# A first piece of w_in asked for earlier, and two of its quarters loaded as 120 and 8 partitions

## The chip, the core and the metric

The kernel runs on one NeuronCore of a Trainium2 chip. Five engines work side by side: PE (matrix products, TensorE), DVE (VectorE), ACT (ScalarE), POOL (GpSimd) and SP (SyncE), and 16 DMA engines move data between the chip's main memory (HBM) and the on-chip memory. DMAs are asked for by POOL (their packets stand in the profile as queue q0, software_dynamic), by SP (q1) and by ACT (q10); all run on the same 16 engines. The metric is the device time of one execution in microseconds (us), the median of several runs.

## What is computed

The inputs are `x` (8 batches, 8 heads, 512 rows, 64 columns), `state` (8, 8, 32, 64), and two weight matrices `w_in` (512 x 2048) and `w_out` (2048 x 512), all fp32. The reference is a cross attention in both directions, whose outputs are stacked and go through a two-layer network:

```python
scores = scale * x @ state.T ;  a = softmax(scores) ;  xread = a @ state
scores2 = scale * state @ x.T ; a2 = softmax(scores2) ; sread = a2 @ x
rows = concatenate([xread, sread])        # heads side by side: 4352 rows of 512
h = rows @ w_in ;  out = maximum(0.01 * h, h) @ w_out
```

## The kernel before, in words

The kernel never forms `xread`: for each batch it computes `M = state @ w_in` per head (`a_m`, line L389, into PSUM tile `pm`, evicted into the bf16 tile `M`), and then the first layer is `M` times the transposed probabilities `aT` (`ff1`, L410; for batch 0 `ff1_0`, L639). The activation is done on the way out of PSUM by ACT into `hT`, and the second layer (`piece`, L438) multiplies `hT` with `w_out_bf`. The output rows are copied to `ysb` and stored.

The order of the instructions on each engine is written out by hand; each engine works through its own list, and semaphores hold it where an operand is not there.

The stretch that matters here is the head, some 25 us at the start, in which batch 0 goes through a path of its own while the weights arrive:

- SP asks for batch 0's `x` in four transfers of 256 KB (`xf`, L65), and ACT for the first two batches of `state` (`st0f`, L59).
- POOL builds the tables of the head: the identity `ident` (`make_identity`), and in one tile `zeroed` (L76) a regrouped identity `identg` (copies L82 and L86) and the four blocks of ones, `ones4` (memsets L91). PE needs `identg` for the transposes of state (L178, `pst`), `ident` for those of `x` (L487, `pxth`), and `ones4` for the row sums (L548, `r`).
- After the tables POOL asks for fourteen transfers in this order: the four column quarters of `w_in` (`load_w_in`, L145; each 1 MB of fp32, written as 512 KB of bf16), rows 0 to 1 of sixteen of `w_out` (L151), the two halves of batch 1's `x` (`x1`, L573, shown in the trace as `x`), `w_out` rows 2 to 3 and 4 to 7, a half of batch 2's `x` (`xl`, L106), `w_out` rows 8 to 11, the other half, and the rest of `w_out`.
- Eight semaphores count these transfers in turn, so POOL's ninth DMA waits until its first has landed, the tenth until the second, and so on.
- DVE casts `xf` to bf16 (L139), PE transposes and multiplies, and the softmax of batch 0 runs over small steps: the maxima (L527), their split into two bf16 parts `hi` (L535) and `lo` (L538), exponentials on ACT (L543), sums (L548), reciprocals (L558), their spread over rows (`qb`, L517) and the product (L566).
- PE's list then has, in this order: `pm` of quarter 0 for batches 0 and 1, `pm` of quarter 1, the first six column blocks of the first layer, `pm` of quarter 2, four more blocks, scores again, `pm` of quarter 3, six more blocks (L639, outputs `php` and `ph`; ACT evicts them in L651 and L647), a first part of the second layer for batch 0 (`pyw`, L438), the transposes of batch 1's `x` (L705, `pxt`, in two groups of eight; DVE has cast `x1` before that, L687), and then the second layer of batch 0 mixed with batch 1's attention.

From there on PE works through batch after batch with hardly a gap.

Of the kernel before, what the change touches and what calls it, by code (L numbers as in the profile page):

```python
# [9 lines left out]
P = 128  # L10
B, H, S, D = 8, 8, 512, 64
NS = 32
DFF = 2048
DM = 512
SROW = S + NS
NT = S // P
NK = H // 2
SCALE = 1.0 / (D ** 0.5)

BF16 = mybir.dt.bfloat16  # L20
# [7 lines left out]
def kernel(  # L28
# [9 lines left out]
    nc = tc.nc  # L38

    consts = ctx.enter_context(tc.tile_pool(name="consts", bufs=1))  # L40
    wpool = ctx.enter_context(tc.tile_pool(name="wpool", bufs=1))
# [27 lines left out]
    warm = consts.tile([P, 2], FP32, name="warm")  # L69
    nc.vector.memset(warm[:], 0.0)  # L70
    nc.scalar.activation(out=warm[:], in_=warm[:], func=AF.Exp)
    ident = consts.tile([P, P], BF16, name="ident")
    make_identity(nc, ident[:])
    NI = 2 * (P - NS)
# [5 lines left out]
    for g in range(2):  # L80
# [6 lines left out]
            identg[:, g, D:].rearrange("p (k q) -> p k q", k=NK), heads[:, 1, :, g]  # L87
        )

    for c in range(NK):  # L90
        nc.gpsimd.memset(ones4[NS * c:NS * (c + 1), c:c + 1], 1.0)  # L91

    w_in_bf = wpool.tile([P, NK, DFF], BF16, name="w_in_bf")
    w_out_bf = wpool.tile([P, 16, DM], BF16, name="w_out_bf")
    xs, xt, xl = {}, {}, {}

    def load_x(b, eng):
# [39 lines left out]
    def cast_x0(q, copy):  # L137
        v = q % 2
        copy(  # L139
            xs[0][q // 2][:, :, 2 * v:2 * v + 2].rearrange("p t h d -> p h t d"),  # L140
            xf[q][:].rearrange("p h (t d) -> p h t d", t=NT),
        )

    def load_w_in(c):
        nc.gpsimd.dma_start(  # L145
            w_in_bf[:, :, DM * c:DM * (c + 1)],
            moe_w_in[:, DM * c:DM * (c + 1)].rearrange("(k p) f -> p k f", p=P),
        )

    def load_w_out_rows(j0, j1):  # L150
        nc.gpsimd.dma_start(  # L151
            w_out_bf[:, j0:j1, :], moe_w_out[P * j0:P * j1, :].rearrange("(j p) f -> p j f", p=P)
        )
# [411 lines left out]
    def probs0(u):  # L565
        nc.vector.tensor_tensor(out=a0.aT[:, u], in0=e10[u][:], in1=qb0[u][:], op=ALU.mult)  # L566

    for c in range(4):
        load_w_in(c)
    load_w_out_rows(0, 2)  # L570
    x1 = [consts.tile([P, NK, 2 * P], FP32, name="x1", tag=f"x1{u}") for u in range(2)]
    for u in range(2):
# [13 lines left out]
    for q in range(2):  # L586
        cast_x0(q, VEC)
        x0_t(q)
        if q == 0:
            st1_evict()  # L590
            spin(1, "py", S // 2)
    scores0(0)
    cast_x0(2, VEC)
    x0_t(2)
    scores0(1)
    cast_x0(3, VEC)
    x0_t(3)
    max0(0)
# [291 lines left out]
```

## Time and profile before

| what | value |
|---|---|
| median of three runs | 217.58 us |
| the three runs | 217.41, 217.58, 219.19 us |
| span of the profiled execution, first to last instruction | 214.6 us |
| PE busy | 206.1 us, 96% of the span |
| TensorE clock granted | full in all 40 slices |

The profile's page gives the profiled execution as its span alone; its full time is not listed beside it. The median is 2.98 us above the span, which is what lies around the first and the last instruction, as far as this execution was like the median one.

In the profile, "DMA" in a bracket behind a row names a transfer that ended the engine's idle time. A row of the timeline holds the start and the length in us, the engine, the line, the operation, what it writes and reads, and how many instructions were merged.

### The profile page before, as it was taken

What the parts mean: (1) busy time and instruction counts of PE and PEld (TensorE: products, weight loads), DVE (VectorE), ACT (ScalarE), POOL (GpSimd) and SP (SyncE); (2) the same over time, 40 slices, a digit from 0 to 9 for tenths busy, and PEclk for the clock granted to TensorE, in tenths of its full rate; (3) what the DMA queues carried; (4) which work ended last, traced back from release to release, by engine and by line L of the source; (5) the groups of instructions that cost most, each with busy time, mean ns of one, the idle gap of its engine ahead of it and who ended that gap; (6) DMA issues with size and microseconds to landing.
All of it is one profiled execution on the core that took longest, in us unless ns stands there. A gap on an engine that the chain in (4) does not pass through costs nothing.

```text
span 214.6 us, 3685 instructions
## 1 busy us (share of the span) xinstructions
PE 206.1 (96%) x1479; PEld 96.5 (45%) x1504; DVE 97.7 (46%) x149; ACT 139.1 (65%) x263; POOL 25.4 (12%) x39
## 2 busy tenths in 40 slices
PE   7789999999999999999999999999999999999993
PEld 2533434344454444444444444444444455466542
DVE  2666687698748235741784095706580000000001
ACT  3578675898788476856696579647774756464420
POOL 8724100030032040521000000000000000000000
PEclk9999999999999999999999999999999999999999
DMA  6999999576992987394216321422124110111113
GB/s 205 207 206 295 257 253 113 126 270 124 241 217 79 200 243 244 89 276 89 87 52 138 59 99 52 100 47 101 48 68 79 74 74 2 49 52 49 49 49 101
DMA packets 38400, 27.70 MB, mean 129 GB/s; under 512 B 24560, under 2 KB 33136, under 8 KB 38384
## 3 DMA queue, kind: packets, MB, share of 16 engines
q1 hardware_dynamic: 32864, 18.95, 35.4%
q0 software_dynamic: 5376, 8.39, 17.4%
q8 instruction: 12, 0.20, 0.4%
q10 hardware_dynamic: 144, 0.13, 0.3%
q14 instruction: 4, 0.03, 0.1%
HBM read 17.30 MB, written 8.91 MB: 122 GB/s over the span
## 4 chain that ended last, share of the span: by engine, by line
PE 86%; DMA 7%; POOL 3%; ACT 1%; issue 1%; DVE 0%; POOLq 0%; ACTq 0%
PE py L438 50%; PE ph L410 22%; DMA x<-in_x_dram 7%; PE ph L421 3%; PE pm L389 3%; PE pyw L438 3%; PE psr L362 2%; PE pyh L462 2%; POOL w_in_bf L145 1%; PE sc L253 1%; ACT M L403 0%; ACT hT L415 0%; POOL x L573 0%; POOL w_out_bf L151 0%; DVE xb L687 0%
## 5 line engine op out<-in xcount | busy, mean ns | idle before, releaser
L438 PE MATMUL py<-w_out_bf,hT 128*128 128x512 bf16 x446 | 116.7, 380 | 1.0
L415 ACT ACTIVATE hT<-ph 128x512 bf16<-128x512 f32 x112 | 66.5, 602 | 41.7 <-PE ph L410 41.0
L438 PEld LDWEIGHTS <-hT 128*128 128x128 bf16 x496 | 46.7, 98 | 57.2 <-issue 5.3
L410 PE MATMUL ph<-aT,M 128*128 128x512 bf16 x221 | 64.9, 379 | 0.2
L410 PEld LDWEIGHTS <-M 128*128 128x128 bf16 x224 | 21.7, 98 | 27.1 <-issue 1.4
L447 ACT COPY ysb<-py 128x512 f32<-128x512 f32 x31 | 18.1, 585 | 10.7 <-PE py L438 10.7
L263 DVE TRANSPOSE_TENSOR_REDUCE mrow<-sc 128x32 f32<-128x1024 f32 x7 | 8.8, 1250 | 33.7 <-PE sc L253 33.7
L467 DVE COPY ysh<-pyh 128x384 f32<-128x384 f32 x1 | 0.6, 557 | 49.0 <-PE pyh L462 49.0
L132 POOL CAST xb<-xl 128x2048 bf16<-128x2048 f32 x5 | 9.4, 1890 | 58.9 <-DMA xl<-in_x_dram 48.2
L285 DVE TRANSPOSE_TENSOR_REDUCE r<-e 128x32 f32<-128x1024 bf16 x7 | 8.7, 1245 | 11.9 <-ACT e L280 11.9
L403 ACT CAST M<-pm 128x1024 bf16<-128x1024 f32 x13 | 13.2, 1013 | 1.2 <-PE pm L389 0.7
L319 ACT ACTIVATE e<-sc,mcol 128x512 bf16<-128x512 f32 x16 | 11.2, 706 | 0.0
L313 DVE TENSOR_REDUCE mcol<-sc 128x2 f32<-128x1024 f32 x8 | 9.7, 1214 | 0.0
L425 ACT ACTIVATE hs<-ph 128x256 bf16<-128x256 f32 x16 | 6.0, 384 | 4.6 <-PE ph L421 4.4
L294 DVE STREAM_TRANSPOSE qb<-qh 128x1024 bf16<-128x1024 bf16 x7 | 8.7, 1245 | 0.2
L271 DVE STREAM_TRANSPOSE mrowb<-mrow 128x1024 f32<-128x1024 f32 x7 | 8.7, 1245 | 0.2
L273 DVE TENSOR_TENSOR sh<-sc,mrowb 128x1024 f32<-128x1024 f32 x7 | 8.6, 1225 | 0.2
L401 DVE CAST M<-pm 128x512 bf16<-128x512 f32 x10 | 6.4, 686 | 4.9 <-PE pm L389 4.9
L403 DVE CAST M<-pm 128x1024 bf16<-128x1024 f32 x7 | 8.5, 1215 | 0.0
L421 PE MATMUL ph<-sr_t,w_in_bf 128*128 128x256 bf16 x64 | 8.3, 273 | 0.0
L438 PE MATMUL pyw<-w_out_bf,hT 128*128 128x512 bf16 x31 | 7.7, 380 | 0.1
L389 PE MATMUL pm<-w_in_bf,st_t 64*32 64x512 bf16 x192 | 7.6, 379 | 0.0
(97 smaller groups left out, 158.0 us busy)
## 6 DMA issues: line engine op xcount, KB each, us to landing
out_dram<-ysb SPq DMA_DIRECT2D x31, 256.0 KB, 2.4
xl<-in_x_dram SPq DMA_DIRECT2D x3, 1024.0 KB, 6.6
w_in_bf<-in_moe_w_in_dram POOLq DMA_DIRECT2D x4, 512.0 KB, 10.4
xl<-in_x_dram POOLq DMA_DIRECT2D x2, 1024.0 KB, 6.7
xf<-in_x_dram SPq DMA_DIRECT2D x4, 256.0 KB, 3.8
w_out_bf<-in_moe_w_out_dram POOLq DMA_DIRECT2D x4, 256.0 KB, 13.9
x<-in_x_dram POOLq DMA_DIRECT2D x2, 512.0 KB, 15.3
w_out_bf<-in_moe_w_out_dram POOLq DMA_DIRECT2D x2, 512.0 KB, 15.4
```

What stands on the lines that cost most here:

```text
L132: nc.gpsimd.tensor_copy(xt[b][:].rearrange("p t h d -> p h t d"), xl[b][:].rearrange("p h (t d) -> p h t d", t=NT),)
L263: nc.vector.tensor_reduce(out=m1[:], in_=flat.rearrange("p (c j) -> p c j", j=NS), axis=AX.X, op=ALU.max, apply_transpose=True,)
L271: nc.vector.transpose(m1b[:], m1[:, :, None].to_broadcast([P, n, NS]))
L313: nc.vector.tensor_reduce(out=a.m2[:], in_=a.sc[:], axis=AX.X, op=ALU.max, negate=True)
L319: nc.scalar.activation(out=a.e2[:, g], in_=a.sc[:, g, :], func=AF.Exp, bias=a.m2[:, g:g + 1], accum_out=a.r2[:, g:g + 1],)
L389: nc.tensor.matmul(at[v][NS * r:NS * (r + 1)], lhsT=st_of(a, g, k), rhs=w_in_bf[D * g:D * (g + 1), k, DM * c:DM * (c + 1)], start=True, st ...
L403: copy(a.M[:, :, cols], pm[:])
L410: nc.tensor.matmul(ph[:], lhsT=a.M[:, g, P * j:P * (j + 1)], rhs=a.aT[:, g, :], start=(g == 0), stop=(g == 1),)
L415: nc.scalar.activation(out=hT[:, j, :], in_=ph[:], func=AF.Prelu, scale=1 / SCALE, alpha=0.01)
L421: nc.tensor.matmul(ph[:, :n], lhsT=w_in_bf[:, k, P * j:P * (j + 1)], rhs=sr_t[:, k, :], start=(k == 0), stop=(k == NK - 1),)
L438: nc.tensor.matmul(y.py, lhsT=hT[:, j, P * i:P * (i + 1)], rhs=w_out_bf[:, j, :], start=(j == 0), stop=(j == 15),)
L447: copy(ysb[:], ys[b, i].py)
```

## The change

`w_in_bf` and `w_out_bf` are created before the tables, and `load_w_in` takes ranges of row blocks (k), partitions (p) and columns (f). Quarter 0 is now loaded in three transfers: 128 partitions by 256 columns of row block 0, asked for by POOL before `make_identity`; the other 256 columns of that block and the row blocks 1 to 3, asked for after the copies of the tables and ahead of the four memsets of `ones4`. Quarters 1 and 2 are each loaded in two transfers, partitions 0 to 119 and partitions 120 to 127. Quarter 3 is loaded as before. So POOL issues eighteen DMAs in the head where there were fourteen: eight for `w_in`, then the same ten as before in the same order. The eight semaphores are now all taken by `w_in`, and the first transfer of `w_out` waits for the first piece, the halves of `x1` for the second and the third, and so on. The instructions on PE, ACT, DVE and SP are the same and in the same order.

```diff
+    w_in_bf = wpool.tile([P, NK, DFF], BF16, name="w_in_bf")
+    w_out_bf = wpool.tile([P, 16, DM], BF16, name="w_out_bf")
+    wv = moe_w_in.rearrange("(k p) f -> p k f", p=P)
+
+    def load_w_in(c, k0=0, k1=NK, p0=0, p1=P, f0=0, f1=DM):
+        cols = slice(DM * c + f0, DM * c + f1)
+        nc.gpsimd.dma_start(w_in_bf[p0:p1, k0:k1, cols], wv[p0:p1, k0:k1, cols])
+
+    load_w_in(0, 0, 1, f1=DM // 2)
     ident = consts.tile([P, P], BF16, name="ident")
     make_identity(nc, ident[:])
...
+    load_w_in(0, 0, 1, f0=DM // 2)
+    load_w_in(0, 1)
     for c in range(NK):
         nc.gpsimd.memset(ones4[NS * c:NS * (c + 1), c:c + 1], 1.0)
 
-    w_in_bf = wpool.tile([P, NK, DFF], BF16, name="w_in_bf")
-    w_out_bf = wpool.tile([P, 16, DM], BF16, name="w_out_bf")
...
-    def load_w_in(c):
-        nc.gpsimd.dma_start(
-            w_in_bf[:, :, DM * c:DM * (c + 1)],
-            moe_w_in[:, DM * c:DM * (c + 1)].rearrange("(k p) f -> p k f", p=P),
-        )
...
-    for c in range(4):
-        load_w_in(c)
+    for c in range(1, 3):
+        load_w_in(c, p1=P - 8)
+        load_w_in(c, p0=P - 8)
+    load_w_in(3)
     load_w_out_rows(0, 2)
```

## The prediction

> **What bounds the kernel now.** I read the page first: whether an engine is full over the whole span, and what the chain that ended last is made of.
>
> ```profile
> span 214.6 us, 3685 instructions
> PE 206.1 (96%) x1479; PEld 96.5 (45%) x1504; DVE 97.7 (46%) x149; ACT 139.1 (65%) x263; POOL 25.4 (12%) x39
> PE 86%; DMA 7%; POOL 3%; ACT 1%; issue 1%; DVE 0%; POOLq 0%; ACTq 0%
> ```
>
> PE is full, and the change takes no work from it. What can move is the 10% of the chain that is DMA and POOL. The chain in order of time, cut to the first 30 us, says where that lies:
>
> ```profile
> 2.89 3.09 POOL w_in_bf L145 x4
> 7.40 15.65 DMA x<-in_x_dram
> 23.07 0.69 DVE xb L687
> 23.82 0.62 PE pxt L705 x8
> 27.10 2.32 PE py L438 x10
> ```
>
> The second half of `x1` is asked for at 7.40 and lands 15.65 us later, at 23.05. DVE casts it, PE transposes it at 23.82, and behind that PE runs on. So the change is worth what it moves the second `pxt` group. The timeline of PE, and that of ACT, give the waits ahead of it:
>
> ```profile
> 12.76 0.41 PE L389 MATMUL pm<-w_in_bf,stbd 64*32 64x512 bf16 x8 [0.24 <-DMA w_in_bf<-in_moe_w_in_dram]
> 14.20 1.67 PE L639 MATMUL ph<-aT,M 128*128 128x512 bf16 x7
> 16.39 0.41 PE L389 MATMUL pm<-w_in_bf,stbd 64*32 64x512 bf16 x8 [0.52 <-DMA w_in_bf<-in_moe_w_in_dram]
> 17.62 1.04 PE L639 MATMUL ph<-aT,M 128*128 128x512 bf16 x4
> 18.58 0.41 PE L253 MATMUL sc<-xT,stbd 64*32 64x512 bf16 x8
> 17.80 1.02 ACT L651 ACTIVATE hT<-php 128x1024 bf16<-128x1024 f32 x1 [0.42 <-PE php L639]
> 20.35 1.02 ACT L651 ACTIVATE hT<-php 128x1024 bf16<-128x1024 f32 x1 [0.55 <-PE php L639]
> 21.27 2.06 ACT L647 ACTIVATE hT<-ph 128x512 bf16<-128x512 f32 x4
> 22.89 0.61 PE L705 MATMUL pxt<-ident,xb 128*128 128x128 bf16 x8
> ```
>
> PE waits for quarter 1 (0.24), for quarter 2 (0.52) and for `x1`. How the transfers come in is read from the DMA view by window, in its count of packets under 512 B: each DMA engine ends its share of a transfer with a tiny mark. The four rows are the windows 7.8:8.7, 9.7:9.9, 12.9:13.8 and 15.4:15.6; the last row is the instruction queue in 12.5:14.
>
> ```profile
> DMA packets 191, 0.18 MB, mean 200 GB/s; under 512 B 15, under 2 KB 191, under 8 KB 191
> DMA packets 39, 0.04 MB, mean 195 GB/s; under 512 B 1, under 2 KB 39, under 8 KB 39
> DMA packets 186, 0.18 MB, mean 195 GB/s; under 512 B 15, under 2 KB 186, under 8 KB 186
> DMA packets 40, 0.04 MB, mean 195 GB/s; under 512 B 2, under 2 KB 40, under 8 KB 40
> q8 instruction: 1, 0.02, 3.7%
> ```
>
> Fifteen engines are through with quarter 0 by 8.7, the sixteenth only at about 9.8; with quarter 2 fifteen by 13.8, while the last mark falls between 15.4 and 15.6 (the other there belongs to a fast engine that is already through with quarter 3). One engine is some 1.2 us late from the first quarter on and about 2 us late after a 0.02 MB instruction fetch has gone through one engine between. A transfer counts as landed when its last engine is done: PE's wait for quarter 2 ends at 16.39, some 2 us after the other fifteen.
>
> **What the change can give back.** Take the late engine out of the way and see what is late next. The wait for quarter 1 goes: 0.24. The first `ph` run ends at 14.20 + 1.67 = 15.87, and quarter 2's products start at 16.39; without a wait such a group starts a little before the run ahead is drained (the scores at 18.58, where the run ahead ends at 17.62 + 1.04 = 18.66: 0.08), so 0.52 + 0.08 = 0.60 is there. For the second `pxt` group, ACT is next: it must have emptied the PSUM tile, which its row ends at 21.27 + 2.06 = 23.33, so the group could start at 23.38 instead of 23.82: 0.44. ACT can follow, since it is idle for 0.42 and 0.55 in this stretch. Sum: 0.24 + 0.60 + 0.44 = 1.28 us, the most that the head can give. Behind it, `w_out` rows 4 to 7 are due: this DMA row, of the issue at 10.46, gives 16.2 us to landing.
>
> ```profile
> w_out_bf<-in_moe_w_out_dram POOLq DMA_DIRECT2D x1, 512.0 KB, 16.2
> ```
>
> It lands at 26.7; the chain's run of ten from 27.10 is two matmuls on older rows and eight on these, so they are needed at 27.10 + 2 x 0.23 = 27.56. That is 0.9 us of slack, enough for a gain below that, and the late engine's delay falls there too.
>
> **The split quarters.** Quarter 2 as 120 and 8 partitions takes the late engine out if shares go by partition, eight to an engine, and the late engine is the one with partitions 120 to 127. It then has nothing to do in the transfer of 120. Its saving per quarter, from the rate of the stream:
>
> ```profile
> 4.00:5.00 1.00, 0.92 (x13) 0.51 (x13) 0.47 (x1) 0.23 (x1) 1.00 (x2) 1.00 1.06 374
> 8.00:9.00 1.00, 0.18 (x4) 0.25 (x4) 0.73 (x3) 0.01 (x1) 0.92 (x2) 1.00 1.23 203
> 2.00:3.00 1.00, 1.00 (x4) 0.43 (x3) 0.00 (x0) 0.67 (x2) 0.89 (x9) 1.00 0.78 192
> ```
>
> The last number is GB/s written. At 203 GB/s an engine writes a 1 KB row of `w_in` in 1024 x 16 / 203 = 81 ns; a quarter is 512 such rows, 32 to an engine, 2.6 us. Sparing it twice saves 5.2 us against a lag of about 2: enough. The price is the eight partitions: 32 rows per quarter, on eight engines four each, 2 x 4 x 81 ns = 0.65 us on those engines. The fifteen prompt engines then set the landing of `x1`: 23.05 less some 2 plus 0.65 is 21.7, and the cast of 0.69 ends at 22.4, ahead of the 23.38 at which ACT lets PE go on. So on the DMA side nearly the whole 1.28 comes in reach.
>
> No row numbers the engines. The Trainium skill ("DMA: Bandwidth & Descriptors", section "Latency and other measured facts") says that engines 7 and 15 are usually slower than the others. The trace agrees that it is one engine, but shows it late, not slow: its marks for quarters 0 and 2 lie 5.7 us apart and the others' windows 5.1, with a fetch between. By that rule alone the late engine would be the last share's in one case of two, which would make the gain below an even bet.
>
> **The first piece.** Its 128 rows of 512 B are read as 1 KB each, 8 to an engine. Beside `xf`, which moves 374 GB/s in 4:5, a read of 1 KB costs an engine 44 ns, so the piece delays `xf` by at most 0.35 us; it delays it by nothing if it falls into the window 2:3, where the engines move only 192 GB/s. Every step of batch 0's softmax hangs on `xf`, as this row of DVE shows for the last of the four. Queue q0 has no row in the window 4:5; its row in 5:6 stands first below, so its first packets come over 2 us after its first issue at 2.83, and a piece issued near 0.7 would move at about 3, at the edge of the free window. I take 0.2.
>
> ```profile
> q0 software_dynamic: 75, 0.08, 47.7%
> 6.46 0.46 DVE L139 CAST xb<-xf 128x512 bf16<-128x512 f32 x1 [0.24 <-DMA xf<-in_x_dram]
> 2.40 0.49 POOL L91 MEMSET zeroed<- 32x1 bf16 x4
> 2.83 3.15 POOL L145 DMA_DIRECT2D w_in_bf<-in_moe_w_in_dram x4
> 8.14 0.78 POOL L151 DMA_DIRECT2D w_out_bf<-in_moe_w_out_dram  x1
> 10.46 0.78 POOL L151 DMA_DIRECT2D w_out_bf<-in_moe_w_out_dram  x1 [1.54 <-DMA w_in_bf<-in_moe_w_in_dram]
> 4.28 0.44 PE L178 MATMUL pst<-zeroed,stb 128*64 128x96 bf16 x8
> 10.54 0.25 PE L548 MATMUL r<-zeroed,e 128*128 128x4 bf16 x4
> 7.74 0.48 DVE L535 CAST hi<-m 128x16 bf16<-128x16 f32 x1
> 9.59 0.17 DVE L535 CAST hi<-m 128x16 bf16<-128x16 f32 x1
> ```
>
> A DMA issue takes POOL 3.15 / 4 = 0.79 us. The tables, 0.79 later, end at 2.40 + 0.79 = 3.2, ahead of the `pst` products at 4.28: hidden with 1.1 to spare. `ones4` comes after two more issues, near 5.2, and its row sums start at 10.54. The rest of quarter 0 is issued by 4.8 instead of 3.6, which costs nothing while `xf`, whose last quarter lands just ahead of its cast at 6.46, still fills the engines, and up to 4.8 + 2.2 - 6.4 = 0.6 if packets again come 2.2 us after the start of the issue; the 1.0 that `x1` has in hand above (22.4 against 23.38) covers it. From there the queue holds transfers ahead of their turn: `x1`, now issued tenth and eleventh, goes out by about 11.5, while the four quarters ahead of it keep the stream until 6 + 4 x 2.6 = 16.4 at the earliest, and the waits on the eight semaphores come no closer than that.
>
> What does move is POOL's busy time: with four more issues ahead of `x1` it runs without a break past 10, where the rows show a pause from 8.14 + 0.78 = 8.92 to 10.46. The same `hi` cast took 0.48 at 7.74, under POOL's issues, and 0.17 at 9.59, in that pause. The second one would now take 0.48 too: 0.3 us on the chain to the second probabilities; without the clash nothing. I take 0.3, the row that has the clash. The Trainium skill ("SBUF — State Buffer", section "Who interferes with whom") says that a DVE cast and POOL shut each other out of a shared port, whichever starts second waiting to the end; the two rows agree. By its rule for the casts of `xf` nothing changes, since POOL issues beside them before and after.
>
> Sum: 1.28 - 0.2 - 0.3 = 0.78 us less. From the span of 214.6 this gives 213.8, and with the 2.98 us between span and median, 216.8 us.
>
> **Rivals.** First, that the splits free nobody, because the late engine is another one, or shares do not go by partition. Then `x1` lands at 23.05 or, if that engine gets a share of the eights, 0.65 later, and the 0.5 us lost in the softmax is covered partly by the 0.24 wait: 217.6 to 218.2, say 217.9. For it: the trace does not name the engine. Against it: one engine alone lags, and every other share is in time, so one split at the right place is all that is needed. The Trainium skill ("DMA: Bandwidth & Descriptors", section "Rules for kernel authors") speaks for it: transfers on part of the partitions share the same engines, and small ones are mostly overhead; no row here shows a split transfer.
>
> Second, slower: 120 rows spread badly. If they went to eight engines, fifteen partitions each, an engine would carry 60 rows instead of 32: 28 x 81 ns = 2.3 us more per quarter, 4.5 for both, and `x1` would land at 23.05 - 2 + 4.5 = 25.6, or 27.6 with the late engine among the eight. That is 2.5 to 4.5 us late on the chain: 220.1 to 222.1. It decides as soon as `x1` lands after 23.05, which takes fewer than about eleven engines. For it: 120 is no multiple of 16. Against: fifteen times eight fits.
>
> Third, that the first piece fits into the free window and the `hi` cast meets no issue, so that nothing is given back: the whole 1.28, 216.3.
>
> **How the numbers follow.** The freed stream with its small costs: 0.50, at 216.8 (216.5 to 217.3). The same with no costs: 0.12, at 216.3. Nobody freed: 0.27. Badly spread: 0.08. Waits that are larger than the rows show, with more than 2.2 us of gain: 0.03. A measurement of this kernel tells about 1% from no change. The range takes in the cap with a little of the runs' own scatter (217.41 to 217.58) below, and the first rival with a little above: 216.1 to 218.4. Both signs hold much of the chance; the likeliest case's own range is the one just given. Faster by over 1%, below 215.4: 0.03. Slower by over 1%, above 219.8: 0.08. Within: 0.89.
>
> **What would show it.** The wait of `pm` for quarter 2 should be gone and that for `x1` too, with `pxt` bound by ACT; the second group should start near 23.0. Sixteen marks of quarter 3 should lie within about a microsecond. `hi` should take 0.48 twice. `xf`'s last cast should start at 6.5 to 6.8. I am wrong if one mark still trails by 2 us behind both splits, if `x1` lands past 23, or if the softmax, not the weights, is what PE waits for at 12 us by more than 0.5.

## The result, and the profile after

The changed kernel takes 217.82 us (median of 20 runs, 217.13 to 219.38); the kernel before, run beside it, takes 217.08 (20 runs, 214.96 to 224.54). The ratio is 1.0053, with a 95% interval of 1.0031 to 1.0075: about 0.5% slower, within 1%, where 0.78 us less had been forecast. (Here and below a ratio leaves out, on both sides, the runs over 1.5% longer than the fastest of their kernel, so it is not the quotient of the two medians.) The time lies in the predicted range; its sign is the other one.

The profiled execution of the changed kernel took 217.9 us, with a span of 216.1, so 1.8 us lie around the span. First its page: span, busy times, and the chain that ended last.

```profile
span 216.1 us, 3689 instructions
PE 207.0 (96%) x1479; PEld 97.2 (45%) x1504; DVE 99.4 (46%) x149; ACT 139.0 (64%) x263; POOL 28.4 (13%) x43
PE 85%; DMA 5%; DVE 3%; POOL 2%; ACT 2%; issue 1%; ACTq 0%; POOLq 0%
```

The chain in order of time says which transfer the DMA share is (start, length, what):

```profile
5.74 1.56 POOL w_in_bf L78 x2
7.30 10.02 DMA w_in_bf<-in_moe_w_in_dram
17.31 0.04 issue
17.36 0.61 PE pm L392 x8
23.93 1.15 PE pxt L710 x16
```

The chain went through `x1` before; now it goes through quarter 2 of `w_in`. Its 120 partitions land at 17.31 and PE's products with them start at 17.36; the other eight land at 17.52, and the group takes 0.61 us instead of 0.41. Behind it PE runs without a wait for a transfer. The second `pxt` group ends at 23.93 + 1.15 = 25.08, where it ended at 23.82 + 0.62 = 24.44: the head has become 0.64 us longer. (The spans differ by 1.5 us. Most of the rest lies at the end: from 180 us on the granted clock is 0.98 in this execution and 1.00 in that of the kernel before.) PE's timeline shows the wait ahead of that:

```profile
13.96 0.56 PE L392 MATMUL pm<-w_in_bf,stbd 64*32 64x512 bf16 x8 [0.94 <-DMA w_in_bf<-in_moe_w_in_dram]
15.55 1.68 PE L644 MATMUL ph<-aT,M 128*128 128x512 bf16 x7
17.36 0.61 PE L392 MATMUL pm<-w_in_bf,stbd 64*32 64x512 bf16 x8
23.92 1.16 PE L710 MATMUL pxt<-ident,xb 128*128 128x128 bf16 x16
```

PE waits 0.94 us for quarter 1, which it had at 12.76. The bracket at quarter 2 is gone, but not the dependence: the run of `ph` ahead of it is itself later. Why the weights are late is seen in the windows of 1 us (the last two columns are the DMA engines' mean share and GB/s; the share is the time of all packets over that of 16 engines, and passes 1 because packets of one engine overlap). From 7 us on nearly all of it is `w_in`.

```profile
6.00:7.00 1.00, 0.62 (x8) 0.41 (x8) 0.90 (x2) 0.73 (x3) 1.00 (x2) 1.00 0.90 146
7.00:8.00 1.00, 0.76 (x16) 0.55 (x13) 0.83 (x3) 0.74 (x2) 1.00 (x2) 1.00 0.83 117
8.00:9.00 1.00, 0.58 (x11) 0.32 (x11) 0.82 (x4) 0.33 (x1) 1.00 (x3) 1.00 1.15 123
9.00:10.00 1.00, 0.99 (x40) 0.60 (x39) 0.71 (x2) 0.17 (x1) 1.00 (x2) 1.00 0.78 94
10.00:11.00 1.00, 0.81 (x36) 0.60 (x36) 0.32 (x2) 0.42 (x1) 0.91 (x2) 1.00 1.06 162
```

The stream that ran at 203 GB/s from 8 to 9 before now runs at 94 to 162 for five microseconds, and in four of them the engines are also less busy (0.78 to 1.06 where 1.23 stood). POOL and DVE, whose rows follow from their timelines, are where the smaller predictions can be read:

```profile
1.23 0.71 POOL L78 DMA_DIRECT2D w_in_bf<-in_moe_w_in_dram  x1 [0.79 <-POOLq L879]
3.64 1.36 POOL L78 DMA_DIRECT2D w_in_bf<-in_moe_w_in_dram  x2
4.99 0.75 POOL L102 MEMSET zeroed<- 32x1 bf16 x4
5.68 3.74 POOL L78 DMA_DIRECT2D w_in_bf<-in_moe_w_in_dram  x5
```

```profile
6.10 1.10 DVE L148 CAST xb<-xf 128x512 bf16<-128x512 f32 x2 [0.66 <-DMA xf<-in_x_dram]
8.16 0.17 DVE L538 CAST hi<-m 128x16 bf16<-128x16 f32 x1
9.71 0.43 DVE L538 CAST hi<-m 128x16 bf16<-128x16 f32 x1
```

### The profile page after: what moved, and what is told of

Same layout as the page of the kernel before. It is cut to its first block, busy times and chain, and to the rows that moved or that the text cites. A ratio compares the mean times of both kernels' runs of the same rounds, so it can differ in the third digit from the quotient of the medians.

```text
span 216.1 us, 3689 instructions
## 1 busy us (share of the span) xinstructions
PE 207.0 (96%) x1479; PEld 97.2 (45%) x1504; DVE 99.4 (46%) x149; ACT 139.0 (64%) x263; POOL 28.4 (13%) x43
## 4 chain that ended last, share of the span: by engine, by line
PE 85%; DMA 5%; DVE 3%; POOL 2%; ACT 2%; issue 1%; ACTq 0%; POOLq 0%
PE py L441 47%; PE ph L413 21%; DMA w_in_bf<-in_moe_w_in_dram 5%; PE pyw L441 3%; PE ph L424 3%; PE pm L392 3%; PE pyh L465 2%; PE psr L365 2%; POOL w_in_bf L78 1%; PE ph L644 1%; PE sc L256 1%; PE php L644 1%; DVE r L292 1%; DVE r L288 1%; DVE qb L297 1%
```

## The experiments

Each ratio is against the kernel before on the same chip, run beside it, with its 95% interval; "three pieces" are the 64 KB, 64 KB and 384 KB (as written) of quarter 0.

### One part of the change at a time

**Splits alone.** Quarter 0 whole and behind the tables, quarters 1 and 2 as 120 and 8 partitions.

```diff
-    for c in range(4):
-        load_w_in(c)
+    load_w_in(0)
+    for c in range(1, 3):
+        load_w_in(c, p1=P - 8)
+        load_w_in(c, p0=P - 8)
+    load_w_in(3)
```

> Quarter 0 whole and behind the tables as in the kernel before; only quarters 1 and 2 are split into 120 and 8 partitions. Theory T1 (the small pieces of quarter 0 let the DMA queue run dry, and each restart is late by engine; the splits do lift the late engine): the stream stays at about 200 GB/s from 6 us on, quarter 1 lands by 12, PE has no wait of more than 0.1 for quarters 1 and 2, the second pxt group ends near 23.6 to 23.9 instead of 24.44, ratio 0.995 to 0.998. Theory T2 (the transfers of 120 and 8 partitions themselves are slow to start, so they cost): the rate drops below 150 GB/s when quarter 1 is due, quarter 1 lands after 13, ratio 1.003 or more.

Measured: 216.12 us against 215.83, ratio 0.9997 (0.9964 to 1.0029). The splits by themselves give nothing and cost nothing.

**Pieces alone.** The three pieces as in the change, the first ahead of the tables; quarters 1 to 3 whole.

```diff
+    load_w_in(0, 0, 1, f1=DM // 2)
     ident = consts.tile([P, P], BF16, name="ident")
...
+    load_w_in(0, 0, 1, f0=DM // 2)
+    load_w_in(0, 1)
     for c in range(NK):
...
-    for c in range(4):
+    for c in range(1, 4):
         load_w_in(c)
```

> Quarter 0 in its three pieces with the first ahead of the tables, as in the changed kernel; quarters 1 to 3 whole. T1: the dip to 94 to 160 GB/s between 6 and 11 stays, quarter 1 lands at about 13.7 to 14, the late engine is there as well, quarter 2 lands at 16.5 or later, the second pxt group ends at 25 to 26, ratio 1.003 to 1.008. T2: no dip, quarter 1 lands at 12.7 or before, ratio 0.996 to 1.001.

Measured: 217.75 against 215.83, ratio 1.0081 (1.0043 to 1.0119). The whole loss is here, and the same dip: 165, 158, 109, 61 and 167 GB/s in the windows from 6 to 11. PE waits 0.80 for quarter 1 and has it at 13.81.

**Quarter 0 whole, ahead of the tables.**

```diff
+    load_w_in(0)
     ident = consts.tile([P, P], BF16, name="ident")
...
-    for c in range(4):
+    for c in range(1, 4):
```

> The whole of quarter 0 asked for ahead of the tables in one transfer, quarters 1 to 3 whole behind the tables. It is four times the early bytes of the first piece, so xf is delayed by up to 1.4 us, and the softmax with it. T1 (what counts is that the queue does not run dry): quarter 0 lands by 8, quarter 1 is issued by 4.4 and follows without a dip, so no wait for weights at 12, but softmax later: second pxt group at 24.2 to 25, ratio 0.999 to 1.005. T2 says nothing else for this one; a dip between the early quarter and the others of more than 1 us would speak for another cause, the restart after the tables.

Measured: 219.08 against 215.83, ratio 1.0108 (1.0052 to 1.0164). No dip follows (206 and 209 GB/s from 9 to 11), but quarter 0 and `xf` share the engines from 4 to 9 us, and DVE waits for `xf`:

```profile
7.72 0.67 DVE L146 CAST xb<-xf 128x512 bf16<-128x512 f32 x1 [2.19 <-DMA xf<-in_x_dram]
9.16 0.70 DVE L146 CAST xb<-xf 128x512 bf16<-128x512 f32 x1 [0.76 <-DMA xf<-in_x_dram]
```

This is another way to lose: the last cast of `xf` starts 2.7 us later than at 6.46. Up to 1.4 had been expected, by taking quarter 0 for four times the first piece; its 512 KB are eight times 64 KB, and 8 x 0.35 = 2.8 us would have been close.

**The three pieces in the change's order, but all behind the tables,** the quarters whole.

```diff
-    for c in range(4):
+    load_w_in(0, 0, 1, f1=DM // 2)
+    load_w_in(0, 0, 1, f0=DM // 2)
+    load_w_in(0, 1)
+    for c in range(1, 4):
         load_w_in(c)
```

> Quarter 0 in the same three pieces, but all behind the tables and the ones, so that the issues of w_in follow each other without a gap; quarters 1 to 3 whole. T1 in its strict form (pieces are small, so engines finish them before the next is ready): a dip as in the changed kernel, quarter 1 at 13.5 or later. T1 in its milder form (the dip comes from the gaps between issues, which the tables and the memsets of ones4 make): no dip, quarter 1 at 12.7 to 13.2, ratio 1.000 to 1.003. T2: as before, 12.7.

Measured: 218.01 against 215.83, ratio 1.0084 (1.0047 to 1.0122). So the loss does not need an early first piece. The slow stretch is from 6 to 8 here (94 and 136 GB/s), and it reaches `xf`, which shares the engines: its last cast starts at 7.82, after a wait of 1.55.

### What the kernel before does in another execution

The profile on which the prediction rests is one execution. Here is the kernel before, unchanged, once more, and beside it the splits alone once more (the execution that had been profiled of them was disturbed).

> The kernel before, unchanged, profiled once more. If the late engine of the profile shown (1.2 us from quarter 0 on) belongs to that one execution, the last mark of quarter 0 now comes within 0.6 us of the others, PE's waits for quarters 1 and 2 are under 0.2 together, and the second pxt group ends by 23.9 with a span near 213.6. If it belongs to the kernel, the waits (0.24, 0.52) and the 24.44 are there again.

> The kernel with the splits alone, profiled once more, since the first profile caught an execution in which one quarter of xf came 3.4 us late. T1: no dip below 180 GB/s between 7 and 12, quarter 1 lands by 12, no wait for quarters 1 and 2, second pxt group between 23.3 and 23.9. If the splits cost something of their own, a dip when quarter 1 is due, and PE waiting for it.

Measured: 215.95 us for the kernel before, with a span of 213.9, and 216.54 for the splits, span 213.1. PE's timeline of the kernel before:

```profile
12.67 0.41 PE L389 MATMUL pm<-w_in_bf,stbd 64*32 64x512 bf16 x8
15.76 0.41 PE L389 MATMUL pm<-w_in_bf,stbd 64*32 64x512 bf16 x8
18.18 0.40 PE L389 MATMUL pm<-w_in_bf,stbd 64*32 64x512 bf16 x8
22.13 1.10 PE L705 MATMUL pxt<-ident,xb 128*128 128x128 bf16 x16
```

None of the three waits that the forecast meant to remove is here: no bracket at quarter 1, none at quarter 2, and both `pxt` groups in one run that ends at 23.23. Its chain comes from `xf`, not from the weights or `x1`:

```profile
2.25 4.19 DMA xf<-in_x_dram
6.46 0.46 DVE xb L139
15.82 0.34 PE pm L389 x8
22.14 1.09 PE pxt L705 x16
```

The late engine itself is there in part. These are the windows 7.8:9, 9:9.9, 12.9:14.1 and 14.1:15.6 of the DMA view:

```profile
DMA packets 251, 0.24 MB, mean 201 GB/s; under 512 B 15, under 2 KB 251, under 8 KB 251
DMA packets 181, 0.19 MB, mean 206 GB/s; under 512 B 0, under 2 KB 181, under 8 KB 181
DMA packets 245, 0.24 MB, mean 196 GB/s; under 512 B 15, under 2 KB 245, under 8 KB 245
DMA packets 304, 0.31 MB, mean 207 GB/s; under 512 B 1, under 2 KB 304, under 8 KB 304
```

No mark of quarter 0 trails past 9; of quarter 2 one does, at 14.87 in the trace's record of the semaphore, 0.8 us behind the others at 14.06. But PE asks for it only at 15.76. The 1.2 us that one engine had lost by quarter 0 belonged to the first execution; without them the rest of its delay lies in PE's slack.

Against this execution the changed kernel's head is 25.08 - 23.23 = 1.85 us longer, and not 0.64.

The splits change nothing on this chain: their `pxt` rows end at 22.16 + 1.12 = 23.28. Nor do they spare the engine that is late. These are the times at which the sixteen engines count up the semaphore of a transfer of 120 partitions, in that execution, for quarter 1 and quarter 2:

```
quarter 1:  9.11 | 11.08 11.11 11.12 11.20 11.22 11.22 11.24 11.25 11.26 11.27 11.29 11.31 11.40 11.41 11.47
quarter 2: 12.11 | 12.52 13.77 13.79 13.80 13.93 13.94 14.03 14.04 14.21 14.23 14.34 14.39 14.39 14.48 15.57
```

One engine has no share and is through 2 us ahead of the other fifteen; so 120 partitions do go to fifteen engines. In quarter 2 one of those fifteen is 1.1 us behind the rest: the late engine is another one than the spared.

The trace also shows when an engine falls behind. In this execution a fetch of 16 KB of instructions starts at 12.77 and takes one engine 0.89 us; the last engine was 0.04 us behind the next for the transfer counted ahead of it, and 1.09 for the one on the move. In eleven of the sixteen executions traced, the lag of one engine grows by 0.4 to 1.2 us at such a fetch (0.89 to 0.98 us long, between 12.5 and 15.7). No run moves or removes the fetch, so that it is the cause is argued; but in ten of the eleven no engine was over 0.3 us late ahead of it.

The stream of `w_in` in the second execution of the kernel before, to be set beside the five windows of the changed kernel:

```profile
6.00:7.00 1.00, 0.82 (x13) 0.48 (x13) 0.74 (x3) 0.84 (x3) 1.00 (x2) 1.00 1.25 208
7.00:8.00 1.00, 0.98 (x12) 0.48 (x12) 0.97 (x3) 0.89 (x2) 1.00 (x2) 1.00 1.24 205
8.00:9.00 1.00, 0.19 (x4) 0.25 (x4) 0.73 (x3) 0.00 (x1) 0.92 (x2) 1.00 1.24 201
9.00:10.00 1.00, 0.87 (x40) 0.51 (x36) 0.82 (x2) 0.30 (x1) 0.77 (x1) 1.00 1.24 208
10.00:11.00 1.00, 0.97 (x44) 0.73 (x52) 0.18 (x1) 0.43 (x2) 0.01 (x1) 1.00 1.24 204
```

The sums are 1026 KB here and 146 + 117 + 123 + 94 + 162 = 642 KB in the changed kernel: 384 KB less, or 1.9 us of a stream of 205 GB/s.

### Order, number, or pause

**Large piece first.** The three pieces behind the tables, in the opposite order; nothing else differs from the kernel with the pieces late.

```diff
+    load_w_in(0, 1)
     load_w_in(0, 0, 1, f0=DM // 2)
     load_w_in(0, 0, 1, f1=DM // 2)
-    load_w_in(0, 1)
```

> Quarter 0 in the same three pieces, all behind the tables, but the large one (row blocks 1 to 3) first and the two small ones after it; quarters 1 to 3 whole. Same number of transfers as in the kernel with the pieces late. T1 (small pieces at the head of an empty queue let the engines run dry): no dip in 6 to 9, ratio 0.998 to 1.003. If it is the number of transfers or the small rows as such (rival T3), the dip stays and the ratio is 1.005 or more.

Measured: 216.44 against 216.14, ratio 1.0000 (0.9966 to 1.0033). From 6 to 10 the stream runs at 207, 182, 173 and 204 GB/s. The same three transfers, without a loss: neither their number nor their size decides.

The Trainium skill ("DMA: Bandwidth & Descriptors", section "Rules for kernel authors") says that transfers under 64 KB are mostly overhead and that small ones should be joined. By that rule the 32 KB eights of the splits would cost wherever they stand, and the pieces, 64 KB as written, lie at its edge. The times do not bear it out in this stream: the eights cost nothing that was measured (0.9997), nor did the pieces with the large one in front (1.0000).

**The memsets of `ones4` moved ahead.** The changed kernel, with the four memsets in front of the second and third piece, so that POOL issues from the second piece on without a break.

```diff
+    for c in range(NK):
+        nc.gpsimd.memset(ones4[NS * c:NS * (c + 1), c:c + 1], 1.0)
     load_w_in(0, 0, 1, f0=DM // 2)
     load_w_in(0, 1)
-    for c in range(NK):
-        nc.gpsimd.memset(ones4[NS * c:NS * (c + 1), c:c + 1], 1.0)
```

> The changed kernel with one move: the four memsets of ones4 ahead of the second and third piece of quarter 0, so that POOL issues seven transfers of w_in without a break. If the break of 0.7 us between the third piece and quarter 1 is what lets the queue run dry (T4), the dip at 9 to 10 goes and the ratio is 0.997 to 1.001. T1: the dip stays, since the second and third piece are asked for 0.5 later and the engines are dry by then; ratio 1.003 to 1.008.

Measured: 217.85 against 216.14, ratio 1.0082 (1.0045 to 1.0120). The dip stays (104, 147, 149, 125, 172 from 6 to 11), and PE waits 0.99 for quarter 1 at 13.92. The 0.75 us of memsets between POOL's issues are not the cause.

**The changed kernel with two lines exchanged,** and the changed kernel itself on the same chip.

```diff
-    load_w_in(0, 0, 1, f0=DM // 2)
     load_w_in(0, 1)
+    load_w_in(0, 0, 1, f0=DM // 2)
```

> The changed kernel with its first piece still ahead of the tables, but behind the tables the large piece (row blocks 1 to 3) first and the second small one after it. Theory A (small pieces lose the time because POOL asks for one of 64 KB in 0.79 us, while the stream writes it in 0.33: the large piece at once behind the tables gives the queue enough to write): no dip, q0 at 190 GB/s or more from 7 to 11 us, quarter 1 by 13.0, the ratio within 0.997 to 1.003. Theory B (what costs is that the engines, once started by the early piece, run dry behind it and start again one by one, however large the next piece is): the dip to 90 to 160 GB/s between 6 and 11 stays, quarter 1 lands near 13.9, ratio 1.004 to 1.009.

> The changed kernel once more, beside the others on this chip. If its loss is the dip, it shows the dip again (90 to 165 GB/s between 6 and 11) and a ratio of 1.004 to 1.009; if the loss was that of one set of executions, the ratio is within 0.998 to 1.002 or the dip is not there.

Measured: 216.67 with the exchange, 217.46 without, 216.66 for the kernel before: ratios 1.0002 (0.9963 to 1.0040) and 1.0055 (1.0011 to 1.0098). The windows from 7 to 10 with the exchange:

```profile
7.00:8.00 1.00, 0.76 (x16) 0.55 (x13) 0.83 (x3) 0.78 (x2) 1.00 (x2) 1.00 1.20 190
8.00:9.00 1.00, 0.58 (x12) 0.32 (x10) 0.78 (x4) 0.30 (x1) 1.00 (x3) 1.00 1.29 193
9.00:10.00 1.00, 0.96 (x40) 0.57 (x38) 0.75 (x2) 0.21 (x1) 1.00 (x2) 1.00 1.22 196
```

(From 11 to 12, where the eights of quarter 1 pass, this execution has a short dip to 138 GB/s; the splits alone had 204 there. PE then waits 0.47 for quarter 2, whose last engine is done at 16.38, 1.2 us behind the next.) The unexchanged kernel has 170, 116 and 95 GB/s in them, much as in its first profile (117, 123, 94). PE has quarter 1 at 12.79 with the exchange and at 13.95 without. The intervals of the two ratios overlap; the ten runs of each differ by 0.95 us on average (216.75 and 217.70). Theory B (engines started by the early piece run dry and start again one by one, whatever comes next) falls: the early piece and the pause behind it are still there. What the two lines decide is whether a small piece is asked for right before the large piece of its quarter.

That a short transfer stands ahead of a long one is not enough. With the exchange the second small piece stands directly ahead of quarter 1, with the large piece first both do, and in the splits the eights stand directly ahead of quarters 2 and 3; none of these kernels lost time that was measured.

### What a small piece does there

Theory A gave a reason: POOL asks for 64 KB in some 0.7 us, the stream writes it in a third of that, and the queue runs dry. The next run tests the reason by giving quarter 1 the three pieces, behind a whole quarter 0.

```diff
+    load_w_in(0)
+    load_w_in(1, 0, 1, f1=DM // 2)
+    load_w_in(1, 0, 1, f0=DM // 2)
+    load_w_in(1, 1)
+    for c in range(2, 4):
```

> The kernel before with quarter 0 whole and quarter 1, the second in the queue, in the same three pieces, the small ones first. Theory that small pieces cost where the queue is empty: behind quarter 0 they wait in a queue with 2.6 us of work in it, so no dip (q0 200 GB/s or more from 6 to 11), ratio within 0.997 to 1.003. Theory that three transfers for a quarter cost by themselves wherever they stand (their marks, their issues of 0.79 us, x1 asked for two turns later): the dip comes one quarter later, between 9 and 12, quarter 1 lands near 13.9, ratio 1.005 to 1.009.

Measured: 217.52 against 216.66, ratio 1.0047 (1.0001 to 1.0092; the interval nearly touches 1). The profiled execution, at 216.31, is not longer than the kernel before, and quarter 1 lands at 12.61 in it, not near 13.9. But the dip is there, one quarter later:

```profile
8.00:9.00 1.00, 0.42 (x24) 0.44 (x24) 0.60 (x4) 0.03 (x1) 0.78 (x2) 1.00 1.18 133
9.00:10.00 1.00, 1.00 (x55) 0.61 (x47) 0.69 (x3) 0.51 (x1) 0.60 (x1) 1.00 0.96 80
10.00:11.00 1.00, 1.00 (x48) 0.52 (x36) 0.36 (x2) 0.65 (x3) 0.63 (x2) 1.00 1.23 200
```

POOL had issued these pieces between 3.7 and 5.7, 2.5 us or more before. So theory A has the effect of the order right, and its reason wrong: the stream slows although the pieces had long been asked for. The last three kernels vary the piece, all in the kernel before with quarter 0 behind the tables: row block 0 in one piece of 128 KB and then the other three; two equal halves by columns; and small, large, small.

```diff
+    load_w_in(0, 0, 1)
+    load_w_in(0, 1)
```

> The kernel before, quarter 0 behind the tables in two pieces: row block 0 with all its 512 columns (packets of 1 KB, 128 KB written), then the row blocks 1 to 3. If a short piece ahead of a long one is what costs, whatever its packets: a dip (q0 under 160 GB/s in one or more of the windows 5 to 11), ratio 1.003 to 1.008. If it is the pieces with packets of 512 B ahead of the long one: 195 GB/s or more from 6 to 11, ratio 0.997 to 1.003.

```diff
+    load_w_in(0, f1=DM // 2)
+    load_w_in(0, f0=DM // 2)
```

> The kernel before, quarter 0 behind the tables in two equal halves by columns, all four row blocks in each, all its packets 512 B. If packets of 512 B ahead of longer ones cost: a dip as in the changed kernel, near the end of quarter 0 or behind it, ratio 1.003 to 1.008. If it is the short piece that costs: none here, both halves are 32 packets to an engine as a whole quarter is; only packets of 60 ns for 512 B instead of 98 for 1 KB, which makes quarter 0 some 0.5 us longer; ratio 0.999 to 1.003.

```diff
+    load_w_in(0, 0, 1, f1=DM // 2)
+    load_w_in(0, 1)
+    load_w_in(0, 0, 1, f0=DM // 2)
```

> The kernel before, quarter 0 behind the tables as small piece, large piece, small piece. One small piece directly ahead of the large one, as in the changed kernel, but nothing ahead of the tables and no pause in the queue. If that neighbourhood is enough: a dip, ratio 1.003 to 1.008. If it takes two small ones in a row: none, 190 GB/s or more from 6 to 11, ratio 0.997 to 1.003.

Measured, against 215.87: block first 218.84, ratio 1.0147 (1.0115 to 1.0179); halves 217.05, 1.0036 (1.0003 to 1.0069); small, large, small 217.95, 1.0094 (1.0061 to 1.0127). The first and the last had four runs each. One short piece in front is enough, and packets of 512 B are not needed: with the block first all are 1 KB, and it is the slowest of the three. Its windows, and its cast of the last quarter of `xf`:

```profile
6.00:7.00 1.00, 1.00 (x13) 0.80 (x12) 0.10 (x1) 0.77 (x3) 1.00 (x2) 1.00 0.90 29
7.00:8.00 1.00, 0.10 (x2) 0.00 (x0) 0.00 (x0) 0.47 (x1) 1.00 (x3) 1.00 0.90 90
8.00:9.00 1.00, 0.00 (x0) 0.00 (x0) 0.15 (x1) 0.00 (x0) 0.83 (x3) 1.00 1.16 188
```

```profile
8.85 0.43 DVE L145 CAST xb<-xf 128x512 bf16<-128x512 f32 x1 [2.75 <-DMA xf<-in_x_dram]
```

From 6 to 7 the packets take 0.90 x 16 = 14.4 us together and write 29 KB: 0.50 us for a packet of 1 KB, where the whole quarter takes 1.24 x 16 / 201 = 0.099 us per KB (the row 8:9 of the kernel before). So here the packets themselves are slow, rather than missing. In the changed kernel it is both: in 8:9 they take 1.15 x 16 / 123 = 0.15 us per KB, and in 9:10 0.78 x 16 / 94 = 0.13, with the share down to 0.78 from 1.24. The halves, a little slow throughout (192, 152, 189 and 173 GB/s from 6 to 10), lie between.

The trace's records of single packets tell the pieces (512 B) from the rest (1 KB). With the large piece first a packet of a small piece takes 60 ns, never more. In the kernels with the pieces late and with the pieces of quarter 1 it takes 83 to 114 ns on average in the slow windows: there the short pieces themselves are slow. In the changed kernel the second small piece passes at 60 ns, and the large one behind it is slow: a 1 KB packet takes 130 ns on average from 6 to 9 us, and up to 1.56 us, against 98 in the splits alone.

In the kernels with short pieces directly behind the tables the slow packets meet `xf` on the same engines, and its last cast starts at 7.82, 7.30, 8.06 and 8.85 instead of 6.46 (pieces late, halves, small-large-small, block first). They lose their time at the start of the softmax; the changed kernel, whose pieces come as `xf` ends, loses it at quarter 1. What all kernels with the loss share is a short piece, over all 128 partitions, asked for right before the rest of the same quarter. What makes the packets slow or late then stays open: it is neither POOL's rate of issue, nor the packet size, nor the number of transfers. The addresses (one block of 128 rows read by all engines at once) were not varied by themselves, and a short piece at the head of the stream followed by a transfer of another quarter was not tried.

## Why the prediction was wrong

**The waits that were to go** (0.24, 0.60 and 0.44, sum 1.28). The reading of that one execution was right; that the next ones would have them was assumed. In the second execution of the kernel before none of the three is there. Such waits come and go: for `x1` one of 0.38 stands in the execution with the large piece first, without splits, one of 0.36 in that with the two lines exchanged, with splits, and one of 0.34 in the second execution of the changed kernel. The splits alone measure 0.9997 (0.9964 to 1.0029); a gain of 1.28 us would be 0.994, so it was not to be had. With it falls the use of 2.98 us between span and median: it set a profiled span beside a median of other executions. The changed kernel has 217.9 - 216.1 = 1.8, the kernel before 215.95 - 213.9 = 2.05. Only because of that surplus does the forecast of 216.8 look near; in the span it said 213.8, and 216.1 came.

**The rest of quarter 0** ("costs nothing", or up to 0.6 us, "the 1.0 that `x1` has in hand above covers it"). This is the step that failed by sign. It counted when the packets would start and took for granted that the stream then ran at its 203 GB/s. It ran at 94 to 162 from 6 to 11, 1.9 us of stream lost, so that PE has quarter 1 at 13.96 instead of 12.76, after a wait of 0.94. And the cover named was the wrong one: quarter 1, needed at 12.7, and quarter 2, needed at 15.8, are asked for by PE long before `x1`. The runs show this step as the cause: pieces alone lose (1.0081), and the exchange of two lines takes the loss away (1.0002 against 1.0055), as the large piece in front does where all three are behind the tables (1.0000 against 1.0084).

**The split quarters.** The spread was right: fifteen engines with a share and one without, in the counts above, and a stream of 207, 202, 209 and 200 GB/s from 7 to 11. The Trainium skill ("DMA: Bandwidth & Descriptors", section "Why a DMA increments its semaphore by 16 and not by 1") says that such a copy asked for by POOL can put as many partitions on an engine as partitions divided by 16, rounded up: eight for 120, so fifteen engines. The counts agree. The rival of badly spread rows, which needed 4.5 us more, is out. What failed is the condition that the late engine be the one with partitions 120 to 127: in the execution counted, the one without a share is 2 us ahead, and another one trails by 1.1. In most executions the lag first appears at the instruction fetch, which the forecast had seen and taken for an addition of 0.8 us to a lag that was there from the first quarter on; which share the fetch hits is not known.

**The first piece** (`xf` later by 0.2, at most 0.35). Right: the last cast ends at 6.10 + 1.10 = 7.20 instead of 6.92, 0.28 later. POOL's first issue started at 1.23, not near 0.7.

**The tables** (hidden) and **the casts of `hi`** (0.48 twice). The tables cost nothing visible. The second `hi` took 0.43 instead of 0.17, as predicted, but the first lost its clash and took 0.17. It was no cost either, since the kernel before has the clash in the other execution too: 0.48 and 0.39.

**The rivals.** That the splits free nobody gave 217.9 us, the measured time, and its condition is the one that the counts show. But it met the time by luck, for its sum is not what happened: it had half a microsecond lost in the softmax, and the time went in the pieces. Of the signs named, the second half of the `pxt` run came at about 24.5 instead of 23.0, and PE waits for a transfer at quarter 1 instead. `x1` lands at 23.69, past the 23 that was to show the forecast wrong; PE no longer waits for it in this execution, as it reaches that group a microsecond later itself (23.92 instead of 22.89).

## What to carry to other kernels

A wait for a transfer, read in a single execution, is a candidate and not yet a gain: look at a second execution before a change is built on a late engine. When a load is cut up so that its first part comes sooner, read what the rest of the stream does afterwards: wherever a short piece of a quarter was asked for right before the rest of that quarter, this stream fell below 170 GB/s for 2 to 5 us (29 to 144 in its worst one, of some 205); with the large piece first the same pieces cost nothing that was measured. The cover for a late load is the slack of the first consumer behind it, not of the last.

## What the runs showed of the hardware

- One engine is 0.4 to 1.2 us behind the others in quarter 2 or 3 of most profiled executions, split or whole; in the first one it was 2 us. In eleven of the sixteen it appears or grows as a 16 KB instruction fetch takes one engine 0.89 to 0.98 us.
- A packet of 1 KB took 0.50 us on average in one stretch, five times its usual 0.099. In that microsecond only packets of `w_in` started, none of `xf` and no instruction fetch; what else the memory had to serve, the trace does not show.
- A stretch in which PE was little busy was followed by one at half clock. With the block first, these are the windows 7.1:10.5 and 10.5:13.9, PE's busy time in front and the granted clock third from the end:

```profile
7.10:10.50 3.40, 0.84 (x13) 0.59 (x13) 1.58 (x6) 0.96 (x2) 2.40 (x4) 1.00 1.13 170
10.50:13.90 3.40, 3.15 (x85) 2.33 (x91) 1.32 (x6) 1.07 (x2) 0.99 (x2) 0.50 1.24 207
```

The Trainium skill ("TensorE: Matmul & The Clock Gate", section "Part 1: The HAM clock gate (the "warmup" mystery)") says that an idle window of about 3.4 us takes the clock to half. The length agrees: the clock's record has half from 10.50 to 13.91. That the window be idle does not: PE was still busy for 0.84 of the 3.4 us ahead of it. So a transfer that is late by 2 us in the head can cost more than its own wait. Half clock stands in the profiles of the pieces late, the halves, small-large-small and the memsets moved too (3.4 us each), and of quarter 0 ahead of the tables (6.8 us), but in neither profile of the changed kernel; those ratios hold a part that is not the transfer's own.
